# Splitting a two-bank PSUM tile one head pair earlier, with the order of issue fitted anew

## The chip, the cores and the metric

The kernel runs on one core of one Trainium2 chip. The metric is the device time of one execution in microseconds (us). Each comparison gives the median of several runs. The profile comes from one execution of its own, so its time is named beside the median.

## The reference

Three layers follow each other. The first is attention over 32 heads (4 batches of 8) with 576 positions and 64 columns: a pooled part over means of four positions, and a local part with a mask. The second is a feed-forward layer with softplus, the third one with `h * cos(h)`.

```python
out_d = sm_attn(q_d, k_d, v_d)                # q, k, v averaged over groups of four
out_up = np.repeat(out_d, factor, axis=2)     # factor = 4
mask = np.abs(pos[:, None] - pos[None, :]) < factor
scores = np.where(mask, scale * np.matmul(q, k.transpose(0, 1, 3, 2)), -1000000000.0)
...                                           # row softmax of scores, with 1e-09
x = out_up + np.matmul(attn, v)               # as 2304 tokens x 512
...
h = x @ w_in                                  # 512 x 2048
g = np.maximum(h, 0.0) + np.log1p(np.exp(-np.abs(h)))
x = g @ w_out                                 # 2048 x 512
...
h = x @ w_in2
out = (h * np.cos(h)) @ w_out2
```

## The kernel before

Attention goes over 16 head pairs. The first four pairs, p00 to p03, are those of the first batch; p10 is the first pair of the second one. Its stages on TensorE are A, the local scores (L933, L939), B, the pooled scores (L1013 to L1040), C, the transposes of the local weights (L1095), D, those of the pooled weights (L1116, L1120), and E, the products with the values (L1162, L1167, L1199). Between A and C, VectorE takes the maximum `nm` (L965), subtracts it (`sm`, L591), sums (`rs`, L978) and scales, and ScalarE takes the exponential (L975). Between B and D, ScalarE takes the exponentials with their sums (`ed`, L1063). After E of a pair, VectorE adds the two parts of its output into `raw` (L1223), which is the MoE's input: one block of 128 columns for each pair, so four blocks make the input of the first 512 tokens.

The weights of MoE 1 come as 1 MB blocks into two buffers `stg` (L731, issued by SP). Block by block ScalarE rebases the bits (L744), VectorE joins them (L765, or L588 and L752), and ScalarE takes bounds (L787). MoE 1 first multiplies six of its sixteen units in f32 (L1392, `first_in`): a unit needs one product for each of the four blocks `raw`, and then ScalarE (L1401, L1405, L1409) and VectorE (`g`, L1413) make softplus of it. The scales of weights and inputs go through a transpose on TensorE (L629) and a maximum on VectorE (`red`, L635). All other units run in f16, in three products for each (L1456, L1724). MoE 2 (L1500, L1826) follows from about 425 us on.

PSUM is eight banks. At the start they are four tiles of two banks each, the slots `BANK`, written `any`; all stages of attention draw from them. `halve(0, ...)` (L1858 to L1873) takes one of these tiles away and puts two single-bank tiles in its place, `h0` and `h1`, the slots `HB`. The operation claims a free tile and is ordered after the operations named in its second argument; `outs_of` lists the stages E in the order of the pairs. `first_in` needs the name `halve0` (L1398), so no unit of MoE 1 can start before the split. A second split for MoE 2 stands at L1735.

The order of all instructions is made while the program is built. A planner (`Plan.order`) gives each operation a due time, worked back from the end, adds the offset that the table `MOVES` (L85) has for its name (L355), and then issues by a list rule: of the operations that can start on a free engine, the one that is due first. The instructions of each engine stand in the program in that order, and the DMAs stand in one queue that SP issues. Where TensorE would have nothing to do, in the first 350 us of the planner's time, the planner puts in a filler (`filler`, L2206 to L2218): a matmul of zeros, L2215, into a free `h` if there is one, else into a free `any`. So fillers are fixed instructions like all others.

## Time and profile before

| what | value |
|---|---|
| three runs, us | 828.96, 828.73, 827.40 |
| median, us | 828.73 |
| the profiled execution, us | 827.2 |
| its span on the core, us | 825.4 |
| TensorE's products busy | 811.2 us, 98%, 6970 instructions |
| VectorE busy | 736.4 us, 89% |
| ScalarE busy | 524.9 us, 64% |
| DMA engines' share, main queue | 51.6% |
| granted clock | 1.00 |

The span is the time between the first and the last instruction of the profiled execution; 1.8 us of its time lie around it. Engines are named PE (TensorE's products), PEld (its weight loads), DVE (VectorE), ACT (ScalarE), POOL and SP. A busy share says how long an engine was at work, not whether the work was of use: a filler counts as busy. In a timeline a row that ends in square brackets names the idle time ahead of the instruction and what it waited for. One product of 128 rows in f32 shows as two matmuls, so "x8" at L1392 is four products.

### The profile page before, as it was taken

Reading aid. Unit: us, or ns where it says so; the run is one execution under the profiler, and the core shown is the slowest. Engines: PE = TensorE matmul, PEld = TensorE weight load, DVE = VectorE, ACT = ScalarE, POOL = GpSimd, SP = SyncE. Lnnn points to the kernel's source line nnn. Section 1 sums busy time; section 2 is a strip of 40 time slices with the busy share of each in tenths; the row PEclk is TensorE's granted clock in tenths of the full one; section 3 lists DMA queues with packets and bytes.
Section 4 is the critical chain, followed back from the end, with each engine's and each line's share of the span. In section 5 each row is a group of like instructions: output and inputs, shape, how many; then the busy total and the mean of one; then the engine's idle time right before and its main releaser. Section 6 shows DMA issues by size and latency. Waiting matters only on the chain.

```text
span 825.4 us, 17050 instructions
## 1 busy us (share of the span) xinstructions
PE 811.2 (98%) x6970; PEld 554.5 (67%) x6970; DVE 736.4 (89%) x1473; ACT 524.9 (64%) x877; POOL 1.8 (0%) x9
## 2 busy tenths in 40 slices
PE   8989999999999999999999999999999999999997
PEld 3644454555555544444447888888888888888886
DVE  7989989988695679999898999999999999999773
ACT  5887899554233359798997767665645555646420
POOL 0000000000000000000000000000000000000000
PEclk9999999999999999999999999999999999999999
DMA  9987421112200025775674532545666684689574
GB/s 356 348 311 259 162 97 34 41 53 94 80 17 2 1 104 176 233 228 186 235 275 160 216 135 91 178 154 207 231 227 218 222 287 153 251 266 335 183 215 177
DMA packets 49790, 148.54 MB, mean 180 GB/s; under 512 B 3888, under 2 KB 22960, under 8 KB 45616
## 3 DMA queue, kind: packets, MB, share of 16 engines
q1 hardware_dynamic: 49712, 147.46, 51.6%
q8 instruction: 54, 0.88, 0.4%
q14 instruction: 24, 0.20, 0.1%
HBM read 128.04 MB, written 19.40 MB: 179 GB/s over the span
## 4 chain that ended last, share of the span: by engine, by line
PE 79%; ACT 7%; DMA 6%; DVE 6%; issue 1%; POOL 0%; DVEq 0%; ACTq 0%; SPq 0%; POOLq 0%
PE h L1500 20%; PE any L1826 19%; PE any L1724 19%; PE h L1456 16%; DMA stg<-w1i 2%; DMA stg<-w2i 1%; PE any L1199 1%; DMA stg<-w1o 1%; DMA xt<-scr_out 1%; ACT w1i_t L787 1%; PE any L1095 1%; ACT tab L1658 1%; PE any L939 1%; ACT tab L1670 1%; DMA vd<-vd 1%
## 5 line engine op out<-in xcount | busy, mean ns | idle before, releaser
L1456 PE MATMUL h<-xt,w1i_t 128*128 128x512 f16 (+1 forms) x888 | 179.9, 356 | 0.3 <-DVE red L635 0.3
L1724 PE MATMUL any<-g,w1o_t 128*128 128x512 f16 (+1 forms) x792 | 161.6, 353 | 0.2 <-DVE g L599 0.2
L1456 PEld LDWEIGHTS <-w1i_t 128*128 128x128 f16 x888 | 86.0, 98 | 82.9 <-issue 2.9
L1724 PEld LDWEIGHTS <-w1o_t 128*128 128x128 f16 x888 | 85.5, 98 | 79.5 <-issue 2.0
L1500 PEld LDWEIGHTS <-ri 128*128 128x128 f16 x1194 | 116.7, 98 | 13.9 <-DMA ri<-scr_in 0.2
L1826 PEld LDWEIGHTS <-w1i_t 128*128 128x128 f16 x762 | 74.5, 98 | 11.3 <-issue 2.8
L1500 PE MATMUL h<-tx,ri 128*128 128x256 f16 x636 | 81.7, 273 | 0.0
L1826 PEld LDWEIGHTS <-w1o_t 128*128 128x128 f16 x750 | 73.3, 98 | 8.8 <-issue 0.3
L1500 PE MATMUL h<-xt,ri 128*128 128x256 f16 x558 | 74.5, 273 | 0.0
L1826 PE MATMUL any<-ro,w1i_t 128*128 128x256 f16 x489 | 73.0, 273 | 0.9 <-DVE g L1785 0.5
L609 ACT ACTIVATE w1o_t<-gf 128x512 f16<-128x512 f32 (+1 forms) x68 | 39.5, 587 | 52.4 <-DVE gf L591 34.2
L1651 ACT ACTIVATE tab<-h,i 128x512 f32<-128x512 f32 (+1 forms) x64 | 39.6, 631 | 50.7 <-PE h L1456 46.5
L1826 PE MATMUL any<-ro,w1o_t 128*128 128x256 f16 x435 | 66.8, 273 | 0.1
L591 DVE TENSOR_TENSOR hs<-h,hs 128x512 f32<-128x512 f32 (+1 forms) x96 | 56.9, 595 | 0.9 <-PE h L1500 0.4
L609 ACT ACTIVATE w1i_t<-gf 128x256 f16<-128x256 f32 (+2 forms) x82 | 39.8, 506 | 26.1 <-DVE gf L591 13.0
L591 DVE TENSOR_TENSOR gf<-gf 128x256 f32<-128x256 f32 (+2 forms) x120 | 55.1, 471 | 0.2
L1826 PE MATMUL any<-xt,w1o_t 128*128 128x256 f16 x315 | 48.0, 273 | 0.0
L591 DVE TENSOR_TENSOR w1i_t<-gf,w1i_t 128x256 f16<-128x256 f32 (+2 forms) x91 | 46.2, 523 | 0.5 <-ACT w1i_t L609 0.4
L599 DVE SCALAR_TENSOR_TENSOR g<-tab,sg,g 128x512 f16<-128x512 f32 (+1 forms) x64 | 43.2, 680 | 2.6 <-ACT g L603 1.8
L591 DVE TENSOR_TENSOR w1o_t<-gf,w1o_t 128x512 f16<-128x512 f32 (+1 forms) x69 | 43.2, 634 | 0.9 <-ACT w1o_t L609 0.7
L1826 PE MATMUL any<-xt,w1i_t 128*128 128x256 f16 x273 | 42.9, 273 | 1.0 <-ACT g L603 0.4
L1785 DVE SCALAR_TENSOR_TENSOR g<-any,ik,g 128x512 f32<-128x512 f32 (+1 forms) x35 | 23.8, 693 | 18.6 <-PE any L1826 18.5
(236 smaller groups left out, 1376.2 us busy)
## 6 DMA issues: line engine op xcount, KB each, us to landing
ri<-scr_in SPq DMA_DIRECT2D x31, 896.0 KB, 4.8
ro<-scr_out SPq DMA_DIRECT2D x41, 512.0 KB, 4.8
xt<-scr_out SPq DMA_DIRECT2D x29, 512.0 KB, 5.7
qk<-qk SPq DMA_DIRECT2D x16, 589.0 KB, 4.7
stg<-w1i SPq DMA_DIRECT2D x8, 1024.0 KB, 6.7
stg<-w1o SPq DMA_DIRECT2D x8, 1024.0 KB, 5.6
stg<-w2o SPq DMA_DIRECT2D x8, 1024.0 KB, 5.6
stg<-w2i SPq DMA_DIRECT2D x8, 1024.0 KB, 5.7
```

What stands on the lines that cost most here:

```text
L591: eng[e].tensor_tensor(out=out, in0=in0, in1=in1, op=op)
L599: nc.vector.scalar_tensor_tensor(out=out, in0=raw, scalar=s, in1=other, op0=ALU.mult, op1=op)
L609: nc.scalar.activation(out=out, in_=in_, func=AF.Copy)
L787: nc.scalar.activation(out=out().rearrange("p (m e) -> p m e", m=2), in_=self.floats(b), func=AF.Abs, accum_out=self.bd[:, b : b + 1],)
L939: nc.tensor.matmul(pa.t[64 * h : 64 * h + 64, j, 64 * g : 64 * g + 64], tk.t[64 * j : 64 * j + 64, 0, q0 + 3 : q0 + 67], tk.t[64 * j : 64 ...
L1095: nc.tensor.transpose(pc.t[:, k, 128 * o : 128 * o + 128], sm.t[:, g, :, :].rearrange("p j k -> p (j k)"), ident)
L1456: nc.tensor.matmul(h.t[:, 0:n], l, r, start=(i == 0), stop=(i == 11))
L1500: nc.tensor.matmul(h.t[:, a : a + m], l, r, start=(i == 0), stop=(i == n - 1))
L1651: act(n, 1, True), lambda: nc.scalar.activation(out=x(), in_=h.t[:, 0:n], func=AF.Softplus, scale=col(o.i1, f)),
L1724: nc.tensor.matmul(a.t[:, i, 0:n], l, r, start=(first and j == 0), stop=(last and j == 2))
L1785: dve(256 * m, False, 1), lambda: nc.vector.scalar_tensor_tensor(out=o.t[:, 0 : 256 * m], in0=view(k), scalar=T[t].ik, in1=x.t[:, 0 : 256 ...
L1826: nc.tensor.matmul(a.t[:, z, 256 * c : 256 * c + 256], l, r, start=(b == 0 and x == 0), stop=(b == NB - 1 and x == 2),)
```

## The change

The split of the first two-bank tile is ordered after E of the first head pair where it was ordered after E of the second. The table of offsets, `MOVES`, is replaced as a whole: 148 lines become 159. Nothing else is changed; behind the table, a line of the kernel before stands 11 lines later in the changed one.

```diff
 MOVES = {
-    "L1 0 0 ln#1": -314.5, "L1 0 1 exp#1": 70, "L1 0 1 mm#1": 963, "L1 0 10 G#1": 1002.5, "L1 0 10 abs#1": 29.5,
...
+    "L1 0 0": -382, "L1 0 1 mm#1": 714.5, "L1 0 10 mm#1": 1053.5, "L1 0 11 mm#1": 1026.7, "L1 0 11 relu#1": 1023,
...
-        halve(0, outs_of[1:2])
+        halve(0, outs_of[0:1])
```

The first place is TensorE's queue from the pooled scores of p03 to E of p02, where the first product of MoE 1 stands (`raw_166` is the first block). Before:

```order
L1040 MATMUL any_92<-qd_121 32x144 x4
L2215 LDWEIGHTS zero
L2215 MATMUL h_627<-zero 128x512
L2215 LDWEIGHTS zero
L2215 MATMUL h_627<-zero 128x512
L1392 MATMUL h_627<-raw_166,w1i_t 128x512
L1162 MATMUL any_87<-aTd_132,vs_124 64x144 x2
```

After the change:

```order
L1044 MATMUL any_88<-qd_121 64x144 x4
L1051 MATMUL any_88<-qd_121 32x144 x4
L1403 MATMUL h_531<-raw_166,w1i_t 128x512
L2226 LDWEIGHTS zero
L2226 MATMUL h_532<-zero 128x512
L1173 MATMUL any_87<-aTd_132,vs_124 64x144 x2
```

The first product stands behind the pooled scores with no filler between, and a filler that stood ahead of it stands behind it. Further up, behind E of p00, there are five fillers in both programs: before, all go into `any` tiles; now one goes into an `any` tile and four into the new single bank.

The second place is ScalarE's queue and VectorE's around the softmax of p10. `w1i_t<-stg_109` is the rebase of the sixth weight block loaded, `ed_128` are p10's exponentials. ScalarE before:

```order
L1058 ACTIVATE nd_239<-nd_239 128x3
L603 ACTIVATE aTd_133<-any_87,both_a 128x128
L603 ACTIVATE aTd_133<-any_87,both_b 128x2x16
L1063 ACTIVATE ed_128,rs_235<-any_88,nd_239 128x144
L1063 ACTIVATE ed_128,rs_235<-h_628,nd_239 128x144
L1063 ACTIVATE ed_128,rs_235<-any_88,nd_239 128x144
L744 ACTIVATE w1i_t<-stg_109 128x1024
L975 ACTIVATE sm_126<-sm_126 128x640
L603 ACTIVATE up_135<-any_92 128x144
```

ScalarE after the change:

```order
L1069 ACTIVATE nd_239<-nd_239 128x3
L620 ACTIVATE aTd_133<-any_87 128x288
L614 ACTIVATE aTd_133<-any_87,both_a 128x128
L614 ACTIVATE aTd_133<-any_87,both_b 128x2x16
L755 ACTIVATE w1i_t<-stg_109 128x1024
L1074 ACTIVATE ed_128,rs_235<-any_92,nd_239 128x144
L1074 ACTIVATE ed_128,rs_235<-h_532,nd_239 128x144
L1074 ACTIVATE ed_128,rs_235<-any_92,nd_239 128x144
L614 ACTIVATE up_135<-any_88 128x144
L986 ACTIVATE sm_126<-sm_126 128x640
```

The rebase stands ahead of the three exponentials where it stood behind them, and the copy `up` stands ahead of the exponential `sm`. VectorE before, where `sm_126<-any_88,nm_231` are the two halves of p10's subtraction and `raw_169` is the fourth block of the MoE's input:

```order
L591 TENSOR_TENSOR qd_121<-qt_119 128x288
L965 TENSOR_REDUCE nm_231<-any_88 128x10
L591 TENSOR_TENSOR qt_119<-qk_111 128x576
L591 TENSOR_TENSOR sm_126<-any_88,nm_231 128x3x128
L591 TENSOR_TENSOR qd_120<-qt_119 128x288
L591 TENSOR_TENSOR sm_126<-any_88,nm_231 128x2x2x64
L752 SCALAR_TENSOR_TENSOR w1i_t<-stg_110,w1i_t 128x1024
L978 TENSOR_REDUCE rs_235<-sm_126 128x10
L1223 TENSOR_TENSOR raw_169<-any_92,up_135 128x512
```

VectorE after the change:

```order
L602 TENSOR_TENSOR vs_123<-vd_115 128x192
L763 SCALAR_TENSOR_TENSOR w1i_t<-stg_110,w1i_t 128x1024
L602 TENSOR_TENSOR qd_121<-qt_119 128x288
L976 TENSOR_REDUCE nm_231<-any_92 128x10
L602 TENSOR_TENSOR qt_119<-qk_111 128x576
L602 TENSOR_TENSOR sm_126<-any_92,nm_231 128x3x128
L602 TENSOR_TENSOR qd_120<-qt_119 128x288
L602 TENSOR_TENSOR sm_126<-any_92,nm_231 128x2x2x64
L1234 TENSOR_TENSOR raw_169<-any_88,up_135 128x512
```

The join `w1i_t<-stg_110` stands ahead of the subtraction where it stood behind it, and `raw_169` stands straight behind the subtraction's second half, ahead of the sum `rs_235`. On TensorE the f32 products around that block are exchanged too: the five that end ahead of C of p10 were two that use the first two blocks, then three of which the first uses `raw_169`; now one stands ahead of the product that uses `raw_169`.

The third place is TensorE's queue around the transpose `am` of the input's maxima (L629, L640 in the changed program), which `red` follows on VectorE. Before, from the last two products ahead of it:

```order
L1392 MATMUL h_627<-raw_167,w1i_t 128x512
L1392 MATMUL h_627<-raw_168,w1i_t 128x512
L1392 MATMUL h_627<-raw_169,w1i_t 128x512
L629 LDWEIGHTS am_243
L629 MATMUL h_628<-ident_s,am_243 128x128
L1392 MATMUL h_628<-raw_166,w1i_t 128x512
L1392 MATMUL h_628<-raw_167,w1i_t 128x512
L1392 MATMUL h_628<-raw_168,w1i_t 128x512
L1392 MATMUL h_628<-raw_169,w1i_t 128x512
L1162 MATMUL any_92<-aTd_132,vs_123 64x144 x2
L1167 MATMUL any_92<-aTd_132,vs_123 64x144 x2
```

After the change:

```order
L1403 MATMUL h_531<-raw_167,w1i_t 128x512
L1403 MATMUL h_531<-raw_168,w1i_t 128x512
L1403 MATMUL h_531<-raw_169,w1i_t 128x512
L640 LDWEIGHTS am_243
L640 MATMUL h_532<-ident_s,am_243 128x128
L1173 MATMUL any_88<-aTd_132,vs_123 64x144 x2
L1178 MATMUL any_88<-aTd_132,vs_123 64x144 x2
L1210 MATMUL any_88<-aT_130,vw_117 64x58 x14
L1210 MATMUL any_88<-aT_130,vw_117 64x42
L1210 MATMUL any_88<-aT_130,vw_117 64x16
L1210 MATMUL any_88<-aT_130,vw_117 64x42
L1210 MATMUL any_88<-aT_130,vw_117 64x16
```

E of p10 (from `any_92<-aTd_132`, now `any_88<-aTd_132`) stood behind the four products that follow `am`; it stands straight behind `am`, with eight products after it. A filler ahead of the products is gone. Behind the eight products the transposes `bd_w1i` follow: one, then four, then five fillers before; now one, three fillers, four, three fillers. SP's queue keeps its order here but for loads of q and v, and the seventh block of weights, whose load waits for the buffer that the join above frees.

Behind 125 us the order differs in many places by a few rows on each engine. The last product of the hidden layer of MoE 2 stands 201 matmuls from the end, where it stood 180 from it.

## Rows read from the trace of the kernel before

**Rows 1.** Busy time by stretches; columns as in the second line (x instructions)

```profile
core 0: us, PE busy (x) PEld busy (x) DVE busy (x) ACT busy (x) POOL busy (x), PEclk, DMA share, GB/s
0.00:25.00 25.00, 21.68 (x333) 11.59 (x334) 19.09 (x42) 16.15 (x42) 1.77 (x9) 1.00 0.88 338
25.00:50.00 25.00, 23.81 (x294) 14.25 (x294) 24.10 (x48) 19.59 (x51) 0.00 (x0) 1.00 0.95 355
50.00:75.00 25.00, 22.64 (x169) 10.97 (x168) 23.54 (x51) 21.22 (x38) 0.00 (x0) 1.00 0.75 266
...
775.00:825.40 50.40, 45.54 (x412) 39.95 (x409) 25.86 (x69) 10.07 (x25) 0.00 (x0) 1.00 0.59 188
sum 825.40, PE 811.16 PEld 554.47 DVE 736.41 ACT 524.86 POOL 1.77; mean PE 42.69 PEld 29.18 DVE 38.76 ACT 27.62 POOL 0.09
```

**Rows 2.** The same table for the filler's line, L2215, alone

```profile
0.00:25.00 25.00, 11.60 (x37) 3.51 (x37) 1.00 0.88 338
25.00:50.00 25.00, 5.73 (x21) 1.80 (x21) 1.00 0.95 355
50.00:75.00 25.00, 1.63 (x6) 0.54 (x6) 1.00 0.75 266
```

**Rows 3.** Timeline of TensorE: start, duration, line, shape, idle time before and releaser

```profile
22.18 1.25 PE L2215 MATMUL any<-zero 128*128 128x512 f16 x5
...
32.78 1.02 PE L1392 MATMUL h<-raw,w1i_t 128*128 128x512 f32 x2
...
44.57 1.98 PE L1392 MATMUL h<-raw,w1i_t 128*128 128x512 f32 x4
47.75 2.84 PE L1392 MATMUL h<-raw,w1i_t 128*128 128x512 f32 x6 [1.19 <-DVE raw L1223]
50.60 0.74 PE L1095 MATMUL any<-ident,sm 128*128 128x128 f32 x5
...
52.60 3.70 PE L1392 MATMUL h<-raw,w1i_t 128*128 128x512 f32 x8 [0.23 <-DVE g L1413]
56.65 0.22 PE L629 MATMUL h<-ident_s,am 128*128 128x128 bf16 x1 [0.34 <-DVE g L1413]
57.59 3.70 PE L1392 MATMUL h<-raw,w1i_t 128*128 128x512 f32 x8 [0.73 <-DVE red L635]
...
66.67 0.22 PE L629 MATMUL h<-ident_s,bd_w1i 128*128 128x128 bf16 x1 [0.26 <-DVE g L1413]
67.65 0.38 PE L629 MATMUL h<-ident_s,bd_w1i 128*128 128x128 bf16 x4 [0.77 <-DVE red L635]
```

**Rows 4.** Timeline of VectorE around the fourth raw

```profile
22.74 0.68 DVE L1223 TENSOR_TENSOR raw<-any,up 128x512 f32<-128x512 f32 x1
...
43.70 0.56 DVE L591 TENSOR_TENSOR sm<-any,nm 128x384 f32<-128x384 f32 x1 [0.66 <-ACT ed L1063]
...
44.87 1.21 DVE L752 SCALAR_TENSOR_TENSOR w1i_t<-stg,w1i_t 128x1024 int32<-128x1024 int32 x1
...
47.01 0.68 DVE L1223 TENSOR_TENSOR raw<-any,up 128x512 f32<-128x512 f32 x1
...
54.04 0.69 DVE L588 TENSOR_SCALAR w1i_t<-w1i_t 128x1024 int32<-128x1024 int32 x1 [0.64 <-ACT w1i_t L744]
```

**Rows 5.** Timeline of ScalarE, exponentials of p10 and the rebase

```profile
42.47 0.47 ACT L1063 ACTIVATE ed<-any,nd 128x144 f32<-128x144 f32 x1 [0.36 <-DVE nm L965]
...
43.48 0.19 ACT L1063 ACTIVATION_READ_ACCUMULATOR ed<-any,nd 128x1 f32 x1
44.45 1.17 ACT L744 ACTIVATE w1i_t<-stg 128x1024 f32<-128x1024 f32 x1 [0.78 <-DMA stg<-w1i]
45.52 0.72 ACT L975 ACTIVATE sm<-sm 128x640 f32<-128x640 f32 x1
```

**Rows 6.** Timeline of SP's queue, weight loads seven and eight

```profile
46.17 3.95 SPq L731 DMA_DIRECT2D stg<-w1i  x2
```

**Rows 7.** The chain of waits, the load ahead of that rebase: start, duration

```profile
37.23 7.19 DMA stg<-w1i
```

**Rows 8.** The chain of waits, its end

```profile
818.86 2.79 PE any L1826 x24
```

293 rows, old and new, of the table MOVES are left out of this document.

## Prediction

> **What bounds the kernel now.** I read the table of busy time by stretches first, then the same table for the filler's line, then TensorE's timeline where these two show loss, then the other engines' timelines at that place, and last the chain of waits. TensorE sets the end: it is busy for 811.16 of 825.40 us [rows 1]. Its idle time is 14.24 us: 3.32 in the first 25 us, 1.19 and 2.36 in the next two stretches, 4.86 in the last one. Of those 4.86, 825.40 less 821.65 = 3.75 lie behind the last product, which starts at 818.86 and takes 2.79 [rows 1, 8]. So 14.24 - 3.32 - 1.19 - 2.36 - 3.75 = 3.62 us of idle time are left for all of 75 to 821.65. The granted clock is 1.00 in every stretch, which is the upper of the two levels, so no edit here can win or lose by the clock unless TensorE falls idle for longer than before.
>
> Busy time hides a second loss: fillers, which multiply by zero and give nothing. They take 11.60, 5.73 and 1.63 us of the first three stretches [rows 2]. From 44 to 69 us the waste is thus six waits, 1.19 + 0.23 + 0.34 + 0.73 + 0.26 + 0.77 = 3.52 [rows 3], and 1.63 of fillers, 5.15 together. That is the only place near the change where TensorE works on the MoE's products and still waits. Before it, TensorE works ahead of the others; the fillers there are fixed instructions and their removal alone would move nothing, because the first long wait, 1.19 us at 47.75 for the fourth `raw`, is set by others.
>
> Who sets it? The fourth `raw` is made by VectorE at 47.01 for 0.68 [rows 4], behind a subtraction at 43.70 that waited 0.66 for ScalarE's last exponential of head pair p10, which starts at 43.48 [rows 4, 5]. ScalarE then waits 0.78 for a weight load at 44.45 [rows 5], issued at 37.23 and 7.19 us on its way [rows 7]. Three engines and the loads are all close to late here.
>
> **The single banks themselves.** The change frees one two-bank tile after E of p00, which ends at 22.18, in place of after E of p01. Its users are the first products of MoE 1, and the first of them starts at 32.78 [rows 3]. The first `raw` is made at 22.74, 0.68 long [rows 4], so the bank is not the last thing missing for long. But order shows that nothing uses it early: behind E of p00 stand five fillers in both programs, four of them now into the new bank, and the first product still stands behind E of p01 and behind the pooled scores of p03, one filler earlier than before. A filler costs 1.63 / 6 = 0.27 us [rows 2]. Gain of the bank: 0 to 0.27, and I take 0, because the wait of 1.19 at 47.75 swallows every shift of TensorE ahead of it.
>
> On the other side, attention rotates through three two-bank tiles from 22 us on where it had four. The Trainium skill, "Perfetto Trace Analysis", says under Matmuls that independent groups should rotate through different PSUM banks so that one is emptied while the next is filled; by that the earlier split would cost a wait. No row of this trace shows such a wait yet, and the only idle time of TensorE from 25 to 50 us is that 1.19 [rows 1, 3]. I bound the cost by 0 and 1.19, and take 0 for the same reason as above. It would count only if the exponentials of p10 came later by it.
>
> **ScalarE's order at 42 to 46 us, the largest term.** The rebase of load six (`w1i_t<-stg_109`) now stands ahead of the three exponentials of p10; it stood behind them. In the trace it starts at 44.45, released by its load, and takes 45.52 - 44.45 = 1.07 to the next start [rows 5]. The load's issue is not moved, so I let it land when it does now. The exponentials take 43.67 - 42.47 = 1.20 (43.48 + 0.19 is the end). They now start at 45.52 and end at 46.72, and the subtraction that waits for the last of them starts there and not at 43.70: 3.0 us later, with VectorE standing still for some 2.5 of them.
>
> The Trainium skill, "PSUM — Partial Sum Buffer", section "PSUM bank collisions raise a hardware error", says that two engines must not touch one bank and quadrant at a time, reads included, and that the compiler adds a dependency between them. The wait of 0.66 for an exponential that only reads the same scores agrees [rows 4]. By that rule the 3.0 us come with the order; without it the subtraction would not wait at all and this term would be 0.
>
> VectorE has prepared for it. The join `w1i_t<-stg_110`, 1.21 at 44.87 [rows 4], now stands ahead of the subtraction, and `raw` comes straight behind its second half. From the first subtraction to the join it is 44.87 - 43.70 = 1.17, so `raw` starts at 46.75 + 1.17 = 47.92 and ends at 48.60. It ended at 47.69. So the 3.0 us shrink to 0.9: the join and the sum `rs`, 47.01 - 44.87 = 2.14 with a short wait, no longer stand between.
>
> **TensorE behind it.** Now one product of the unit comes ahead of the wait and four behind it; there were two and three. Three take 50.60 - 47.75 = 2.85, so four take 3.8: from 48.65 to 52.45, where C of p10 starts. It was 50.60: +1.85. From C to the products it took 52.60 - 0.23 - 50.60 = 1.77, and a filler of 0.27 is gone: they start at 53.95 (+1.35). Their wait of 0.23 is covered by then, since the product that it hangs on ends only 0.8 to 0.9 later than before, so its release comes at about 53.4. They last 3.7, so the spread `am` starts at 57.65 against 56.65: +1.0, its 0.34 covered as well.
>
> Behind `am` TensorE waited 0.73 for VectorE's maximum. E of p10 now stands in that place. From 57.59 to 66.41 (66.67 less its wait of 0.26) it is 8.82, two sets of products of 3.70 and E, so E takes 1.42. Now: 57.65 + 0.2 + 1.42 + 7.4 = 66.7 for the end of both sets, where the spread `bd_w1i` came at 66.67 [rows 3]. The loss is back to 0.0. The next wait, 0.77, has three fillers in its place (0.8), and three stand where five stood: 0.3 more at most, nothing if the bank that comes next is what is waited for. I count 0.
>
> **Loads.** SP issues load seven at 46.17 [rows 6], when the join frees its buffer. The join ended at 46.08. Now three instructions stand between it and a subtraction for which VectorE was ready at 43.70 - 0.66 = 43.04, so it is done before about 43 and the load can go some 3 us earlier. It feeds the rebase whose end VectorE waited 0.64 for at 54.04 [rows 4]. TensorE does not wait for that block before 69 us, so I price it at 0, between 0 and -0.64.
>
> **The rest.** Behind 125 us the table is reordered in hundreds of places, but a row per wait shows only the 3.62 us of idle time named above that could be won, and about as much that could be lost by new ones. I take 0, bounds -3.6 and +3.6. At the end the last product of the hidden layer now has 21 matmuls more behind it, so a wait near 818 us for VectorE may shrink; I count -0.2. Sum, in the order of the parts: 0 + 0 + 0.0 + 0 - 0.2 = -0.2 on the profiled execution's 827.2 (825.4 of span and 1.8 around it), so 827.0. The three runs before lie 0.2 to 1.8 above the profiled one, the median 1.5; I add 0.7, about half of that, and say 827.7.
>
> **Rivals.**
> 1. Faster. The six waits and fillers of 44 to 69 were what the new order was placed around: if `raw` comes no later than before (load six lands a microsecond or more ahead of 44.42, so that its rebase is mostly out of the way by 43.5), E of p10 then covers 0.73, the 1.19 shrinks, and half of the 5.15 goes, 2.6; with a quarter of the 3.62 behind it, 0.9, it is 827.2 - 3.5 + 0.7 = 824.4. For it: the join moved out of the way is worth 1.2 to VectorE at once. Against: the load took 7.19 with the DMA engines 0.95 busy [rows 1, 7], and its place in the queue is the same.
> 2. Slower. The rebase, waiting for its load at the head of ScalarE's queue, holds up the exponentials, the subtraction, the softmax and C of p10. If what I let VectorE and E of p10 make good is not made good (the maximum behind `am` is late by as much, so that the wait of 0.73 comes again behind E), the whole 3.0 stands: 827.2 + 3.0 + 0.7 = 830.9. It decides from the landing of load six: any landing later than 44.42 adds to it one for one, one a microsecond ahead of it leaves 2.0. For it: row by row, nothing of the wait is hypothetical. Against: TensorE's waits behind it add up to 2.1 and can absorb it.
> 3. The split does not do what it says: the freed bank takes fillers alone. This is within the forecast.
>
> **How the numbers follow.** No measurable change, 0.40; rival 1, 0.35; rival 2, 0.25. A change under 0.2%, 1.7 us, can't be told from none. The likeliest case alone gives 825.5 to 829.7 (the bounds of 1.2, 0.3 and 0.64, and half of those of the rest). With 8 in 10 wanted, the range reaches from 823.8, just past rival 1, to 831.5, just past rival 2.
>
> **What would show it.** The first product still near 32.5; the subtraction of p10 near 46.7 with a wait of 2 us or more for an exponential; the fourth `raw` near 47.9; C of p10 near 52.4; the first `bd_w1i` spread within 0.3 of 66.7; from 125 us the same distance to before at each unit. Wrong if load six lands more than 1 us off 44.4, if the first product moves to before 30, or if new waits of over 1 us appear behind 125.

## The result, and the profile after

The changed kernel is slower. Its five runs are 831.37 to 835.35 us with a median of 834.38; the kernel before beside them has a median of 827.62. The ratio is 1.0069, 95% interval 1.0046 to 1.0092, so the loss is about 5.7 us. Six executions of 1049.87 to 4383.61 us, three of them of the kernel before, are left out of all medians and ratios below. The prediction was 827.7 with a range of 823.8 to 831.5: the time lies outside of it. The profiled execution after took 832.68 us with a span of 830.90, 5.50 more than before.

The first view is TensorE's busy time by stretches, cut into the same places for both kernels, of before first and then of after (columns as in [rows 1]).

```profile
75.00:142.00 67.00, 66.07 (x513) 32.73 (x512) 62.03 (x121) 62.40 (x120) 0.00 (x0) 1.00 0.34 120
142.00:440.00 298.00, 296.99 (x2244) 150.37 (x2243) 252.21 (x540) 193.36 (x288) 0.00 (x0) 1.00 0.36 121
440.00:825.40 385.40, 379.97 (x3426) 334.57 (x3423) 355.43 (x676) 212.14 (x344) 0.00 (x0) 1.00 0.61 209
```

After the change:

```profile
0.00:25.00 25.00, 20.55 (x328) 11.25 (x332) 18.98 (x42) 15.97 (x42) 1.77 (x9) 1.00 0.91 337
25.00:50.00 25.00, 21.73 (x305) 13.49 (x296) 21.53 (x42) 18.47 (x48) 0.00 (x0) 1.00 0.95 354
50.00:75.00 25.00, 22.71 (x170) 11.20 (x169) 23.20 (x52) 21.32 (x37) 0.00 (x0) 1.00 0.72 257
75.00:142.00 67.00, 63.77 (x462) 31.44 (x462) 62.14 (x120) 59.15 (x115) 0.00 (x0) 1.00 0.35 119
142.00:440.00 298.00, 297.93 (x2277) 150.55 (x2272) 252.73 (x538) 196.87 (x291) 0.00 (x0) 1.00 0.36 122
440.00:830.90 390.90, 383.45 (x3452) 337.23 (x3450) 357.33 (x686) 214.04 (x343) 0.00 (x0) 1.00 0.61 206
sum 830.90, PE 810.15 PEld 555.16 DVE 735.91 ACT 525.84 POOL 1.77; mean PE 135.02 PEld 92.53 DVE 122.65 ACT 87.64 POOL 0.29
```

Idle time is the length of a stretch less its busy time. In the first 75 us it rises from 3.32 + 1.19 + 2.36 = 6.87 [rows 1] to 4.45 + 3.27 + 2.29 = 10.01, by 3.14. From 75 to 142 it rises from 0.93 to 3.23 (+2.30), from 142 to 440 it falls from 1.01 to 0.07 (-0.94), and behind 440 it rises from 5.43 to 7.45 (+2.02). The sum is +6.52; busy time is 1.01 lower (0.31 of it are fillers, 18.96 against 18.65), which leaves the 5.5 of the spans. Of the 3.14, 1.13 lie in the first 25 us, ahead of the first product of MoE 1, which stands where it stood, so they delay nothing. So the loss has three places, and only the first is one for which I had worked out a price.

**The first place, 30 to 70 us.** TensorE's timeline after (start, duration, line, shape, idle time before and releaser), which answers to [rows 3]:

```profile
32.60 1.13 PE L1403 MATMUL h<-raw,w1i_t 128*128 128x512 f32 x2
...
43.22 1.24 PE L2226 MATMUL any<-zero 128*128 128x512 f16 x5 [1.14 <-ACT aT L620]
...
49.69 3.70 PE L1403 MATMUL h<-raw,w1i_t 128*128 128x512 f32 x8 [1.13 <-DVE raw L1234]
53.82 0.74 PE L1106 MATMUL any<-ident,sm 128*128 128x128 f32 x5 [0.43 <-ACT tab L1420]
...
58.73 0.22 PE L640 MATMUL h<-ident_s,am 128*128 128x128 bf16 x1
...
60.36 7.13 PE L1403 MATMUL h<-raw,w1i_t 128*128 128x512 f32 x16
68.86 0.22 PE L640 MATMUL h<-ident_s,bd_w1i 128*128 128x128 bf16 x1 [1.36 <-DVE g L1424]
...
70.22 0.38 PE L640 MATMUL h<-ident_s,bd_w1i 128*128 128x128 bf16 x4 [0.50 <-DVE red L646]
```

The first product stands where it stood. From there TensorE falls behind in three steps: a filler that waits 1.14 for ScalarE's copies `aT`, the products that wait 1.13 for the fourth `raw`, and the first `bd_w1i` spread, which comes at 68.86 and not at 66.67 [rows 3] and waits 1.36 for `g`. ScalarE at the same place, answering to [rows 5]:

```profile
41.38 1.13 ACT L755 ACTIVATE w1i_t<-stg 128x1024 f32<-128x1024 f32 x1 [1.81 <-DMA stg<-w1i]
42.42 0.75 ACT L620 ACTIVATE aT<-any 128x384 f32<-128x384 f32 x2
...
45.51 1.16 ACT L755 ACTIVATE w1i_t<-stg 128x1024 f32<-128x1024 f32 x1 [1.51 <-DMA stg<-w1i]
46.56 0.43 ACT L1074 ACTIVATE ed<-any,nd 128x144 f32<-128x144 f32 x1
```

Both rebases wait for their loads, and what stands behind them waits too. In this execution the loads take longer: the issues from 30 to 47 us show for the weight blocks (count, size, median us from issue to landing), before and then after,

```profile
stg<-w1i SPq DMA_DIRECT2D x3, 1024.0 KB, 6.2
```

```profile
stg<-w1i SPq DMA_DIRECT2D x3, 1024.0 KB, 8.2
```

SP's queue after shows what changed around load five (32.98; it was 32.41):

```profile
32.55 0.33 SPq L891 DMA_DIRECT2D vd<-vd  x1
32.98 0.37 SPq L742 DMA_DIRECT2D stg<-w1i  x1
33.44 0.38 SPq L891 DMA_DIRECT2D vd<-vd  x1
```

Two loads of v, 384 KB each, stand straight ahead of the block and straight behind it; before, they were issued at 28.27 and 35.43. That they are the cause is not shown: the median of these three loads is 7.2 to 8.2 in the three profiles with this order (after, head_after, exp_ahead), 6.1 to 7.5 in the eight with before's, and 5.8 to 8.0 in the seven in which load five stands ahead again. Load six, issued at 37.33, takes 8.15 on the chain of waits where it took 7.19 [rows 7], and VectorE's subtraction waits for the exponentials that stand behind its rebase (chain of after: start, duration, what):

```profile
37.33 8.15 DMA stg<-w1i
...
46.56 1.19 ACT ed L1074 x6
...
47.78 0.56 DVE sm L602
```

The third step is VectorE's. Its rows around the `g` that the spread waits for, after,

```profile
62.73 0.69 DVE L1424 SCALAR_TENSOR_TENSOR g<-h,tab 128x512 f32<-128x512 f32 x1 [0.48 <-ACT tab L1420]
...
66.98 1.22 DVE L763 SCALAR_TENSOR_TENSOR w1o_t<-stg,w1o_t 128x1024 int32<-128x1024 int32 x1
68.11 0.69 DVE L1424 SCALAR_TENSOR_TENSOR g<-h,tab 128x512 f32<-128x512 f32 x1
```

and before:

```profile
64.61 1.21 DVE L752 SCALAR_TENSOR_TENSOR w1o_t<-stg,w1o_t 128x1024 int32<-128x1024 int32 x1
...
65.93 0.68 DVE L1413 SCALAR_TENSOR_TENSOR g<-h,tab 128x512 f32<-128x512 f32 x1
```

A join of w1o stands ahead of this `g` in both kernels. What is new is what stands ahead of the join: between the `g` at 62.73 and the one at 68.11 there are four steps that round the MoE's input (`xt<-raw`, 0.48 to 0.75 each), where there was one. VectorE makes the `g` 2.18 later, and the spread is 2.19 later.

**The second place, 134 us.** TensorE after:

```profile
134.00 0.73 PE L1106 MATMUL any<-ident,sm 128*128 128x128 f32 x5 [1.51 <-DVE sm L602]
```

C of p13 waits for its softmax; before it started at 129.72 without a wait. The rest of the 2.30 is C of p11 at 89.26, which waits 1.23 for exponentials (before, D waits 0.62 for them at 86.52), and a wait for `red` at 127.15, 0.48 in place of 0.30.

**The third place, behind 580 us.** Ten short waits of TensorE for a step `g` of VectorE or ScalarE, 0.24 to 0.52 each, 4.01 together, where there were five waits, two of them for loads, with 1.88. Two of them, and VectorE's reading that the second one waits for:

```profile
587.07 0.49 PE L1837 MATMUL any<-ro,w1o_t 128*128 128x256 f16 x3 [0.52 <-DVE g L1796]
...
799.74 0.49 PE L1837 MATMUL any<-ro,w1i_t 128*128 128x256 f16 x3 [0.52 <-DVE g L1796]
```

```profile
798.93 0.75 DVE L1796 SCALAR_TENSOR_TENSOR g<-any,ik,g 128x512 f32<-128x512 f32 x1 [2.24 <-PE any L1837]
```

The reading starts as soon as an accumulator is complete (798.93) and lasts 0.75. The accumulators of this stage lie two in a tile, one in each bank of it (`acc[k]` names a tile and one of its halves). One product of 0.33 stands between the accumulator's last product and the next one into the same tile's other half; that one waits the rest.

### The profile page after: what moved, and what is told of

It reads as the page before. It is cut to its first block, busy times and chain, and to the rows that moved or that the text cites. A ratio compares the mean times of both kernels' runs of the same rounds, so it can differ in the third digit from the quotient of the medians.

```text
span 830.9 us, 17061 instructions
## 1 busy us (share of the span) xinstructions
PE 810.1 (98%) x6970; PEld 555.2 (67%) x6970; DVE 735.9 (89%) x1475; ACT 525.8 (63%) x873; POOL 1.8 (0%) x9
## 4 chain that ended last, share of the span: by engine, by line
PE 83%; DMA 6%; DVE 5%; ACT 4%; issue 1%; POOL 0%; DVEq 0%; SPq 0%; ACTq 0%; POOLq 0%
PE any L1735 21%; PE h L1511 20%; PE any L1837 19%; PE h L1467 18%; DMA stg<-w1o 3%; DMA stg<-w1i 2%; PE any L1210 1%; DVE sm L602 1%; ACT w1o_t L755 1%; PE any L950 1%; DVE g L1796 1%; PE any L1106 1%; DMA vd<-vd 1%; PE any L1127 0%; DVE w1o_t L763 0%
## 5 line engine op out<-in xcount | busy, mean ns | idle before, releaser
L1511 PEld LDWEIGHTS <-ri 128*128 128x128 f16 x1104 | 108.0, 98 | 12.7
L1511 PE MATMUL h<-tx,ri 128*128 128x256 f16 x600 | 76.9, 273 | 0.0
L1511 PE MATMUL h<-xt,ri 128*128 128x256 f16 x504 | 66.8, 273 | 0.0
L620 ACT ACTIVATE w1o_t<-gf 128x512 f16<-128x512 f32 (+1 forms) x65 | 37.7, 583 | 32.9 <-DVE gf L602 22.3
L620 ACT ACTIVATE w1i_t<-gf 128x512 f16<-128x512 f32 (+2 forms) x82 | 40.1, 507 | 28.0 <-DVE gf L1597 12.3
L1837 PE MATMUL any<-xt,w1o_t 128*128 128x256 f16 x294 | 46.1, 272 | 0.2 <-DVE g L1796 0.2
L1837 PE MATMUL any<-xt,w1i_t 128*128 128x256 f16 x294 | 44.8, 273 | 0.8 <-DVE g L1796 0.8
L1511 PEld LDWEIGHTS <-xt 128*128 128x128 f16 x432 | 42.2, 98 | 4.9
```

The costliest lines, as they stand in the source:

```text
L620: nc.scalar.activation(out=out, in_=in_, func=AF.Copy)
L1511: nc.tensor.matmul(h.t[:, a : a + m], l, r, start=(i == 0), stop=(i == n - 1))
L1837: nc.tensor.matmul(a.t[:, z, 256 * c : 256 * c + 256], l, r, start=(b == 0 and x == 0), stop=(b == NB - 1 and x == 2),)
```

## The experiments

In the experiments the planner is replaced by a list of the operations in their order of issue, one in a row: name, engine, slots. With the list of before or of after it is the same program as that kernel. So one row can be moved and nothing else. Names: `vd` loads v, `w1i2 load` is load five and `w1i5 rebase` the rebase of load six; of a head pair, A is the scores, A2 the maximum `nm`, A3 the subtraction, B1 the maximum of the pooled scores, B2 the exponentials `ed`; `G` makes a unit's `g`, `gh` rounds it to f16; `L4 t j b` is product b of column j of tile t at the end of MoE 2. Every run is compared with the kernel before on the same chip, in five rounds.

**Which stretch loses.** Three lists join the two orders at one point.

head_after: after up to the scores of p11, before's order behind.

```diff
 w1i3 rebase#1|act|
+p10 vd#1|sp|1
...
+w1i5 rebase#1|act|
...
-w1i5 rebase#1|act|
```

> The order of issue is written out as a list. Everything up to the local scores of p11 (about 70 us) stands in the changed kernel's order, all behind it in the order of before. Theory A (weight loads 5 and 6 land late and ScalarE's rebases hold up the copies and exponentials behind them): the lag of 2.1 to 2.6 us that the changed kernel has at p11 stays to the end, 829.5 to 830.5. Theory B (what is lost early is made good by waits that were there before, the loss is all made behind 70 us): 827.0 to 828.5. If the list cannot be carried on without new waits: above 831.

Measured: 830.18, ratio 1.0023 (1.0011 to 1.0034).

tail_after: the reverse, before up to the scores of p11, after's order behind.

```diff
-p11 A#1|pe|3,1,1
+p13 sum4#1|dve|
+p21 vd#1|sp|0
+xlo0#4|dve|
+p11 A#1|pe|0,0,1
```

> The reverse: up to the local scores of p11 in the order of before, and all behind it in the changed kernel's order. Theory A: the late part has a loss of its own, 1.5 at 134 us and some 1 behind 575 us, but the 2.1 to 2.6 of the head are gone: 829.5 to 831.0. Theory B: all of the loss stays, 832.5 to 834.5. If the head alone were to blame: 827.0 to 828.0.

Measured: 832.26, ratio 1.0048 (1.0031 to 1.0065). The two add up to 1.0071, the whole loss of 1.0069. Some 1.9 us lie in the head (0.9 to 2.8 by the interval), 4.0 behind it (2.6 to 5.4).

head_after also says more of the head. Its order up to p11 is after's, but load six took 7.2 in its profile and not 8.15:

```profile
57.83 0.22 PE L418 MATMUL h<-ident_s,am 128*128 128x128 bf16 x1
...
59.65 7.18 PE L1181 MATMUL h<-raw,w1i_t 128*128 128x512 f32 x16
68.39 0.22 PE L418 MATMUL h<-ident_s,bd_w1i 128*128 128x128 bf16 x1 [1.56 <-DVE g L1202]
```

`am` comes at 57.83, where the forecast was 57.65, and the products end at 66.83, where it was 66.7. The spread waits 1.56 for `g` all the same. So the wait for `g` does not hang on the late landing of load six that after's profile shows. One thing is left open: 7 of the 12 runs have a mean granted clock of 0.998 or less, with a median of 830.60; the other 5 are at 829.01, and the 14 runs of before with a higher clock are at 827.7. How much of the 1.9 is the waits and how much goes with the clock is not separated.

late_after: before up to the first product of MoE 2's first layer, after's order behind.

```diff
 L1 4 10 gh#1|act|3
-L3 0 0 mm#1|pe|1
 scales#38|dve|
-tlo#8|dve|
```

> The order of before up to the first product of MoE 2's first layer (about 425 us), and the changed kernel's behind it. Theory A: by idle time of TensorE this part costs 1.1 to 1.9 us (ten waits of 0.24 to 0.52 where before has five): 829.0 to 830.2. Rival (these waits are paid back, the late part costs nothing): 827.6 to 828.6. If the granted clock falls behind these waits: above 830.5.

Measured: 833.35, ratio 1.0062 (1.0040 to 1.0083). It can't be read as the share of the late part: its profile has a wait of 1.28 at the join, 462.55, that neither kernel has, and the granted clock falls from 85 to 95 us, in the stretch that is before's. I set it aside.

**The bank alone.** Before's order, with the split behind E of p00; six fillers change their tile.

```diff
 fill|pe|b2
+halve0#1|pool|2
 p00 up#1|act|
...
-halve0#1|pool|2
-        halve(0, outs_of[1:2])
+        halve(0, outs_of[0:1])
```

> The order of before, and the split placed directly behind E of p00 as in the changed kernel: the order on every engine is that of before, only the tile that six fillers write into changes. Theory A (the bank itself is worth nothing, the loss is the order's): within 0.1% of before, 827.3 to 829.0. Rival (one two-bank tile fewer for attention makes it wait): 0.3 to 1.2 us slower and a new wait of TensorE between 22 and 30 us.

Measured: 827.60, ratio 0.9997 (0.9984 to 1.0010). The split itself gains and costs nothing.

**The head.** load_ahead is after with the load of v moved behind load five, exp_ahead is after with the rebase behind the exponentials.

```diff
-p10 vd#1|sp|1
 p03 B1#1|dve|3
...
 w1i2 load#1|sp|1
+p10 vd#1|sp|1
```

> The changed kernel with one instruction moved: in SP's queue the weight load 5 stands ahead of the v load of p10 (384 KB) and not behind it. Theory A: it is issued near 32.4, lands about 1.6 us sooner (0.6 from the issue, 1.05 from 384 KB that no longer go first), E of p03 starts at 42.8 to 43.2 and not 44.39, and the end comes 0.5 to 1.5 us sooner than the changed kernel, 831 to 834 by the median. Rival (the DMA engines are full, so the order within the queue moves nothing): landing within 0.3 us of 41.3, the end as in the changed kernel, 832 to 835.

Measured: 833.64, ratio 1.0068 (1.0049 to 1.0086). The blocks from 30 to 47 us take 7.2 (median) and not 8.2, and the filler at E of p03 no longer waits. Both are so in head_after too, which has not this move, so they are not shown to come of it. Nothing reaches the end: TensorE waits 3.60 for `g` at 70.86, and VectorE ahead of it 1.43 for a rebase of w1o that waited 2.03 for its load.

```diff
-w1i5 rebase#1|act|
 w1i7 load#1|sp|1
...
 p10 B2#1|act|
+w1i5 rebase#1|act|
 p10 A3#1|dve|1
```

> The changed kernel with one instruction moved: ScalarE's rebase of weight block 6 stands behind the three exponentials of p10, as before the change. Theory A: the subtraction of p10 starts when VectorE is free, at 46.4, not 47.78, the fourth raw ends 1.4 sooner, and the end comes 0.7 to 1.4 sooner than the changed kernel. Rival (the late landing alone sets the place): the subtraction stays within 0.4 of 47.78 and the time as in the changed kernel, 832 to 835.

Measured: 832.34, ratio 1.0054 (1.0038 to 1.0070); against after's 1.0069 the intervals overlap, so it shows no gain by itself. In its profile the subtraction waits 0.66 for the exponentials and not 1.36, but the spread waits 1.47 for `g`.

The third part is VectorE's join of w1o, 1.22, straight ahead of the `g` that the spread waits for. head_mended is head_after with the two moves above and this one:

```diff
-w1o1 join2#1|dve|
 L1 0 5 G#1|dve|3
+w1o1 join2#1|dve|
```

> The head of the changed kernel with three moves (weight load 5 ahead of p10's v load, the rebase of block 6 behind p10's exponentials, unit 5's softplus ahead of the join of the first w1o block), and the order of before behind p11. Theory A: the three together give back all of the head's 0.23%: 827.6 to 828.8, within 0.1% of before. Rival (one wait of 1.5 us for the scales stays, and the granted clock falls behind it at times): 829.5 to 830.5 as with no move.

Measured: 827.99, ratio 1.0005 (0.9989 to 1.0022), 0.0018 less than head_after, though the intervals overlap. No loss of the head is left that can be measured. Which of the three moves does it is open: the third was not tried by itself. TensorE of head_mended, the same places as in after:

```profile
43.75 1.39 PE L2004 MATMUL any<-zero 128*128 128x512 f16 x5
...
67.98 0.22 PE L418 MATMUL h<-ident_s,bd_w1i 128*128 128x128 bf16 x1 [0.86 <-DVE g L1202]
...
70.28 0.38 PE L418 MATMUL h<-ident_s,bd_w1i 128*128 128x128 bf16 x4 [1.44 <-DVE red L424]
```

The filler's wait of 1.14 is not there, as in head_after; the wait for `g` is 0.86, in place of 1.56 in head_after, but that for `red` is 1.44 in place of 0.67. A wait taken away at one row shows up at the next. That can be why the first two moves showed nothing by themselves.

**The wait at 134 us.** tail_cast_behind is tail_after with ScalarE's rounding of unit 13 moved behind p13's exponentials.

```diff
-L1 0 13 gh#1|act|
 p13 A2#1|dve|3,3
...
 p13 B2#1|act|
+L1 0 13 gh#1|act|
```

> The kernel with the head of before and the late part of the changed one, with one instruction moved: ScalarE's cast of unit 13's output, which waits for VectorE, stands behind the three exponentials of p13 and not ahead of them. Theory A: the subtraction of p13 starts 1.2 to 1.3 sooner, the wait of 1.51 at 132 us for the scaled scores falls to 0.2 to 0.3, and the time falls by 1.0 to 1.4, from 832.26 to 830.9 to 831.3. Rival (the wait comes back at the next place): the wait goes and the time falls by less than 0.4.

Measured: 831.44, ratio 1.0044 (1.0027 to 1.0061); the wait of 1.51 is still there (132.68). My theory, that the rounding holds the exponentials up, fell. ScalarE and VectorE of that run show who does:

```profile
127.36 0.46 ACT L852 ACTIVATE ed<-any,nd 128x144 f32<-128x144 f32 x1 [2.31 <-DVE s_w1o L377]
```

```profile
126.43 0.82 DVE L754 TENSOR_REDUCE nm<-any 128x10 f32<-128x640 f32 x1
127.16 0.17 DVE L377 TENSOR_SCALAR s_w1o<-s_w1o 128x8 int32<-128x8 int32 x1
...
128.59 0.56 DVE L380 TENSOR_TENSOR sm<-any,nm 128x384 f32<-128x384 f32 x1 [1.26 <-ACT ed L852]
```

The exponentials start right after VectorE's maximum of the local scores ends; these scores lie in one tile with the pooled scores that the exponentials read (126.43 + 0.82 = 127.25; the short step named in the brackets ends beside it); the subtraction waits for the exponentials in turn. That the shared tile makes them follow each other is inferred from this order. So tail_max_ahead moves the maximum ahead, and keeps the rounding behind:

```diff
+p13 A2#1|dve|3,3
 p13 B1#1|dve|3
...
-p13 A2#1|dve|3,3
```

> The kernel with the head of before and the late part of the changed one, with two instructions moved: VectorE's maximum of p13's scores (nm) stands straight behind the scores, ahead of the five instructions that it stood behind, and the cast of unit 13 stands behind p13's exponentials. Theory C, formed after the cast alone moved nothing: the exponentials wait for the maximum, because both read p13's two-bank tile, and the subtraction waits for the exponentials, so the maximum's place sets the chain. The exponentials start at about 124.9 and not 127.4, the wait of 1.51 near 132 us falls below 0.4, and the time falls by 1.1 to 1.5 against the kernel with no move (832.26). Rival (the chain is bound further down, by the sum and the scaling): the wait stays above 1.0.

Measured: 830.18, ratio 1.0033 (1.0018 to 1.0047). TensorE's C of p13 there has no wait:

```profile
125.82 5.34 PE L1245 MATMUL h<-xt,w1i_t 128*128 128x512 f16 x24 [1.15 <-DVE red L424]
131.00 0.71 PE L884 MATMUL any<-ident,sm 128*128 128x128 f32 x5
```

The wait is gone in the profile, but the products ahead of it wait 1.15 for `red`, where they waited 0.33 in tail_cast_behind: `red` stands behind the maximum now. Of the 1.51 that leaves 0.69; in time it is 0.0015 less than tail_after, 1.2 us, though the intervals overlap.

**The late waits.** late_interleave is tail_after with eight products of a unit in the other tile put ahead of the waiting one, two for each of four waits:

```diff
-L4 0 5 3#1|pe|1
 L4 0 6 1#1|pe|0
+L4 0 6 2#1|pe|0
+L4 0 5 3#1|pe|1
```

> The kernel with the head of before and the late part of the changed one, with eight products of MoE 2's second layer moved: at the four places where a product waits 0.52 us for VectorE's reading of the other accumulator in its two-bank tile, two more products of the other tile stand ahead of it. Theory D (a product waits for the reading of the neighbouring bank of its tile, and one product of 0.33 between is too little cover for a reading of 0.75): the four waits go, 1.6 to 2.1 us sooner, 830.2 to 830.7. Rival (the loads or the readings come later by as much, the wait moves on): the sum of the late waits falls by less than 0.7.

Measured: 829.98, ratio 1.0029 (1.0012 to 1.0046). That is 0.0019 less than tail_after, though the intervals overlap. The waits at 587 and 714 are gone. Those at 789 and 800 are not, since there I had put the products two places behind the one that waits.

**All together.** four_moves is after with the three moves of the head and the rounding; all_mended is after with the three, tail_max_ahead's two and the eight late ones. Their rows are those shown above.

> The changed kernel with four instructions moved: weight load 5 ahead of p10's v load, the rebase of weight block 6 behind p10's exponentials, VectorE's softplus of unit 5 ahead of the join of the first w1o block, and the cast of unit 13 behind p13's exponentials. Theory A: 1.0 to 1.4 come back at 134 us, and of the head 0.7 to 1.9, so 1.7 to 3.3 sooner than the changed kernel: 830.0 to 832.7. Rival (the head is bound by the chain of weight loads and their two buffers, whatever the order of ScalarE and VectorE): the spread at 68.9 stays within 0.5 of where it is and only the 1.0 to 1.4 come back, 832.5 to 833.5.

Measured: 833.11, ratio 1.0055 (1.0037 to 1.0074). The intervals overlap with after's.

> The changed kernel with all of these moves: three in the head, two at p13, eight late. If the loss is the sum of these places, 2.0 + 1.4 + 2.0 of the 5.7 to 6.0 come back and the time is 828.0 to 829.3, within 0.15% of before. If each wait that is taken away comes back at the next place, or the granted clock falls behind the waits that stay: 831 to 833.5.

Measured: 830.40, ratio 1.0029 (1.0015 to 1.0043): over half of the loss is back.

late_right_place is all_mended with the four misplaced products put right:

```diff
-L4 3 2 5#2|pe|0
 L4 3 4 1#1|pe|1
+L4 3 4 2#1|pe|1
+L4 3 2 5#2|pe|0
```

> The version with all thirteen moves (830.40), with four of its eight late products moved two to four products further up, so that they stand straight ahead of the products that waited at 785.33 and 796.16 (0.52 and 0.51). If a product into one half of a two-bank tile waits for VectorE's reading of the other half, and two products in between cover it, both waits go and the time is 1.0 us lower, 829.4 (ratio to before 1.0017). If these waits hang on VectorE being late as a whole, they come back on the next products and the time stays at 830.4.

Measured: 829.28, ratio 1.0011 (0.9999 to 1.0024). No wait of 0.51 or 0.52 is left behind 440 us; TensorE's waits there, summed:

```profile
PE any L1615 <- ACT g L392: 1.1, 3, 0.4
PE any L1615 <- DVE g L1574: 0.8, 3, 0.3
```

That is 1.9 in all, as in the kernel before. Two products in between cover the reading of the other half where one did not. The interval lies clear of after's (1.0046 to 1.0092): all these moves together give back 0.58 of the 0.69%.

after_more_moves is late_right_place with two more waits mended, which all_mended shows at 69.64 (1.44) and 88.85 (1.40):

```diff
 L1 0 5 G#1|dve|3
+wmax spread#2|pe|1
 w1o1 join2#1|dve|
+wmax#2|dve|
...
+L1 0 6 mm#1|pe|1
 p11 C#1|pe|0,1
```

> The version before in this call with three more moves: the second spread and its maximum behind the join, and one product of unit 6 ahead of the transposes of p11. Theory: what is left of the loss is a set of single waits, each from two neighbours in the order. Then the waits at 69.64 (1.44) and 88.85 (1.40) shrink to under 0.4 each, and with the late ones gone (1.0) the time is 830.4 - 1.0 - 1.0 - 1.0 = 827.4 (ratio 0.9993, within 0.2% of before). Rival: the last 0.2 to 0.3% is the granted clock that falls behind a wait of over a microsecond in some executions; then the waits go as well but the time stays at 829 or above where the clock still falls, and the mean clock of the runs is 0.998 or less. Second rival: TensorE is behind VectorE at that place, and the waits come back some products later with the same sum.

Measured: 829.29, ratio 1.0017 (1.0004 to 1.0029). A miss: the wait for `red` shrinks to 0.47 (68.43) and that at 88.85 goes, but 0.76 at 69.57 and 0.98 at 91.30 come in their place, and the time does not fall. This is what the second rival said.

**What is left: the clock?** TensorE in late_right_place by single microseconds, around its two waits of 1.85 and 1.44 (columns: stretch, length, busy time and instructions, granted clock, DMA share, GB/s):

```profile
66.00:67.00 1.00, 0.00 (x0) 1.00 0.17 64
67.00:68.00 1.00, 0.21 (x2) 1.00 0.03 10
68.00:69.00 1.00, 0.66 (x4) 1.00 0.00 0
69.00:70.00 1.00, 0.00 (x0) 0.65 0.21 33
70.00:71.00 1.00, 0.90 (x6) 0.50 0.52 147
...
75.00:76.00 1.00, 1.00 (x2) 0.50 0.88 316
76.00:77.00 1.00, 1.00 (x3) 0.94 1.04 426
```

The granted clock falls to 0.50, the lower of its two levels (1.2 of 2.4 GHz), and stays there to 76 us, with TensorE at work from 70 on. Of the 12 runs of this kernel 8 have a mean clock of 0.998 or less, with a median of 829.99; the other 4 are at 828.06. Of before's 29 runs beside it 3 are that low; its other 26 have a median of 828.12. clock_fillers tests whether the clock is the cause: ten more fillers keep TensorE at work in the two waits.

```diff
+fill|pe|b3
...
 wmax spread#2|pe|1
...
+fill|pe|b3
...
 wmax spread#1|pe|1
```

> The version with the late moves at the right places (829.28; 8 of its 12 runs with a mean clock of 0.998 or less, median 829.99, the other 4 median 828.06; of before 3 of 29 runs), with ten more fillers (0.27 each by the profile) in the two waits ahead of and behind the first spread, 67.79 (1.85) and 70.10 (1.44): six and four, of which TensorE has 1.6 and 1.1 us. No useful work is moved. If the rest of the loss is the clock that falls to 0.50 behind these waits (69.4 to 75.9 in that profile), then at most a quarter of the runs show 0.998 or less and the median falls to 828.1, that of before (ratio 1.0000 to 1.0005). If the fallen clock only goes along with a late start of the work, and the time is lost in the waits themselves, it stays at 829.3 (1.0011), whatever the clock shows. If the fillers outlast the waits, it is above 829.3.

Measured: 829.66, ratio 1.0018 (1.0003 to 1.0033). A miss in time. The waits shrink to 0.74 and 0.58 and only 4 of 12 runs have a clock of 0.998 or less, but the median stays. The 8 runs with a higher clock have a median of 828.07, near before's 827.93, yet two runs with a clock of 1.00 took 829.92 and 830.79. So the clock goes along with some of the slower runs (these 4 are at 830.05 to 832.61) but is not shown to be the cause of the last 0.1 to 0.2%. That stays open.

**The kernel before.** before_mended applies the same moves to four waits of the kernel before, at 67.65 [rows 3], 86.52, 765.04 and 794.87.

```diff
 wmax spread#2|pe|1
+wmax#2|dve|
...
+L1 0 9 mm#1|pe|0
 p11 D#1|pe|3,1
...
+L3 4 14 mm#1|pe|3
 L4 3 1 0#2|pe|0
...
+L4 3 6 5#1|pe|3
+L4 3 6 6#1|pe|3
 L4 3 4 1#2|pe|0
```

> The kernel before with four waits of its own mended in the same way: the second maximum straight behind its spread, a product of unit 9 ahead of the pooled transposes of p11, two late products ahead of one that waited 0.52, and one ahead of one that waited 0.45. If the rule found in the changed kernel holds in general, 0.6 + 0.6 + 0.5 + 0.45 = 2.2 us go at most: 825.8 (ratio 0.9974). If waits of this size are only moved on, the time stays within 0.1% of before.

Measured: 827.70, ratio 0.9991 (0.9980 to 1.0002). The two late waits are gone in its profile; the one at 86.52 is back at 92.62 with 0.95, behind another stage. A gain is not shown, and no version of these beats the kernel before by more than can be measured.

## Why the prediction was wrong

**Right:** the bank. The forecast 0 to 0.27 with 0 taken; bank_alone measured 0.9997. The Trainium skill, "Perfetto Trace Analysis", section Matmuls, says that groups should rotate through different banks; from it I had drawn that a tile fewer for attention would cost a wait. The measurement decides: with three tiles from E of p00 on nothing is lost here.

**Right in mechanism, wrong in size:** the chain at 42 to 58 us. Each link came as worked out, and each a little over a microsecond late: the subtraction at 47.78 (46.7), `raw` at 48.95 (47.92), C of p10 at 53.82 (52.45), `am` at 58.73 (57.65). The misses of 1.0 to 1.4 start at the step "The load's issue is not moved, so I let it land when it does now": load six landed at 45.48 and not at 44.42 [rows 5, 7]. The runs do not show that the order did this. In head_after, with the same order, it took 7.2, and the chain came within 0.4 of the forecast. I had gone by one load in one profile and given its landing no range. The subtraction's wait was sized too large: 1.36, and 1.89 in head_after, for 2.5. The exponentials that it waits for read the pooled scores, which lie in the same two banks, and not the same scores, as the prediction has it.

**Wrong:** "The loss is back to 0.0." It rested on the spread `bd_w1i` following the products at once. E of p10 did cover the wait of 0.73 behind `am`: no wait stands there after. But the spread waits for a `g` as well. The prediction took its 0.26 out of the sum and let it be 0, without a reason; VectorE makes that `g` 2.18 later, and the wait grew to 1.36 (1.56 in head_after, where the products end as forecast). I moved TensorE's rows along and left VectorE's as they were. Measured by head_after the head costs 0.23%, 1.9 us, and by head_mended three moves give it back together.

**The step that failed:** "The rest", taken as 0 with bounds of 3.6 either way. tail_after measured 0.48%, 4.0 us (2.6 to 5.4), more than two thirds of the loss and, by the median, past the bound. Its ground, that as much could be lost as was idle before (3.62), is no bound: an order can add waits that were not there. Two mechanisms carry most of it. The maximum of p13, moved behind other work, holds up exponentials, subtraction and C: 1.51 in the profile, which tail_max_ahead took away, at 0.82 more of the wait for `red`. The late products of one tile, interleaved one by one, wait for the reading of its other half: four waits of 0.51 to 0.52, of which late_interleave took away two and late_right_place all; the last two go with 0.18% of the time (1.0029 and 1.0011, intervals overlapping). The second could be read before: by the rows of the changed order, a product into the tile that VectorE reads, with one product in between, and from the trace of before a reading of 0.75 against a product of 0.33; the kernel before has such a wait itself, 0.52 at 794.87. I had looked at the start of the order alone.

The wait near 818 did not shrink as forecast (-0.2): 0.25 before and 0.25 after, at 826.63. The clock was left out of the sum unless TensorE fell idle for longer than before. It did (1.36 and 1.51), and after's two longest runs, 835.03 and 835.35, have the lowest mean clocks of its five, 0.996 and 0.997; what this adds to the loss is not shown. Of the signs of being wrong two came: load six landed more than 1 us off 44.4 in after's profile, and a new wait of 1.51 stands behind 125.

**The rivals.** The faster one failed with the landing of load six, on which it hung: 45.48 in after and some 44.5 in head_after (37.25 + 7.2), not a microsecond ahead of 44.42. The slower one named the right place, by another wait (the maximum behind `am`, where none came), and a price of 3.0 for what costs 1.9. It could not have reached 834 alone; the case that was missing is a loss in the head and one behind it together.

## What to carry to other kernels

When a whole order of issue is fitted anew, its price is not in the part that the change speaks of: go through every stage's rows for two patterns, a reading of an accumulator with less work behind it than it lasts, and a long instruction put ahead of one that another engine waits for. A load that is not moved can land a microsecond later in one execution than in the next, so a landing read from one profile needs a range, and a second profile of the same order should be read before the order is blamed. In a tight pipeline a single mended wait comes back at the next row, so mend and time a whole stretch.

## What the runs showed of the hardware

Loads of 1 MB took different times in the same order of issue. The three issued from 30 to 47 us took 8.2 us (median) in after and 7.2 in head_after, and 6.2 in before and 7.1 in bank_alone. The DMA share from 25 to 50 us was 0.95 in before and in after.

TensorE's granted clock fell to 0.50 behind some waits and not behind others of the same length. In load_ahead it was 0.50 from 71 to 74 us behind a wait of 3.60, in late_right_place from 70 to 76 behind waits of 1.85 and 1.44, in exp_ahead from 72 to 74 behind 1.47 and 0.67. In head_after, with waits of 1.56 and 0.67 at the same place, it stayed at 1.00, and so it did in the profiled execution of after, with 1.36 and 0.50.
